# Attention and feed-forward on one core: late q and k loads by row chunks, four more seven-product blocks, and a written order for the first batch

## The chip, the cores and the metric

The kernel runs on one core of a Trainium2 chip. The metric is the device time of one execution in microseconds (us), the median of several runs. A profiled execution gives the trace from which all durations are read.

## The reference

For 8 batches of 12 heads with 448 rows of 64, attention without softmax; then a feed-forward block with a gate on all 3584 tokens of width 768, inner width 1536:

```python
scores = scale * np.matmul(q, k.transpose(0, 1, 3, 2))      # scale = 1/sqrt(64)
attn = np.maximum(scores, 0.0) ** 2 / S
attn_out = np.matmul(attn, v)                               # then x = (tokens, heads * 64)
g = x @ w_gate
gelu = 0.5 * g * (1.0 + erf(g * inv_sqrt2))
val = x @ w_val
out = (gelu * val @ w_out).astype(np.float32)
```

Inputs and output are float32 in memory; the kernel computes in bfloat16 with float32 sums.

## The kernel before

The Python program plans the whole kernel first and then writes the instructions in the order of the plan. An `Op` is one step on one engine with a planned cost; `run_plan` takes, at each moment of planned time, the next step that is ready on each engine. The chip does not see the plan: each engine runs its instructions in the order that was written and waits on semaphores.

**Matrix products.** Every matmul uses a quarter of TensorE (PE): 64 rows by 64 columns of weights, so four run side by side, and helper `mm` (L343) writes nearly all of them; they must be told apart by their tiles. The widths of the moving operand are 448 (scores, values, gate and value products), 224 (seven-product blocks and some tails) and 384 (output products).

**Attention of a batch.** Heads are taken in thirds of a batch, m = 0, 1, 2, of four heads, and in pairs `pr`. `load_qk` (DMA issued on POOL, L402) brings q and k into `qk16`, cast to bfloat16; `load_v` (L417) brings v. In batches 0 and 1 PE transposes q and k (`add_transposes`, `add_first_transposes`) and DVE copies the result to `qkT`. From batch 2 on, DVE regroups into `qkr` (L449), and two DMA transposes per third, issued on SP (L454), write `qkT`. `add_scores` writes one of 21 score steps of a batch: scores into `sp`, relu on ACT into `rl` (L685), square on DVE into `attnT` (L697). `add_values` multiplies by v and copies to `xT` (L760). In batch 0 transposes, scores and values are in a fixed order, by times that a formula gives; later attention steps are units that the planner places by a time spread from `lo` to `hi`, which `SHIFT` moves for each batch from 2 on.

**Feed-forward of a batch.** For each 128 of the inner width there is a gate product and a value product (24 matmuls of 448 columns each), gelu on ACT (L1007) and a product on DVE (L1012) into `uT`. In `NPB[b]` blocks of a batch the four products of 256 of the inner width are made by seven products of half the tokens' width instead (`add_pair`, names 1 to 7, 24 matmuls of 224 columns each), with sums of weights `ws` (`add_pair_sums`, L833), sums of tokens `ts` (L857), copies and sums of parts (L925, L929), gelu (L933) and product (L938). Weight sums of blocks 4 and 5 are kept in the room of the load tiles, so they come after the last loads and transposes (`ROOM = 4`). A block's weights are overwritten by a sum when its first batch with seven products is reached, so `NPB` can only grow.

**Output.** Groups of four 64-token chunks, a to n, are made by seven products too (`add_product`, names a1 to n7, 384 columns); results go to `osb` (L1185, L1187) and are stored (L1202) from SP, each 64-row chunk by a DMA of its own. The last tile is stored in two halves of its columns.

**Order.** `LINE` lists the feed-forward work: a digit is a gate or value product of that batch, `3A1` product 1 of block A of batch 3, `a1` output product 1 of group a. The position gives a planned time; a unit is taken as soon as it is ready, in the order of these times.

**Loads.** Late q and k (batch 2 on) come in four loads per third, two heads each; v in four loads too. A load waits for a relu step of an earlier third (`PACE`), and starts only behind a mark in PE's instruction stream, one in every 256 instructions (`gate`, `Blocks`).

Of the kernel before, what the change touches and what calls it, by code (L numbers as in the profile page):

```python
# [9 lines left out]


LINE = """
0 0 0 0 0 0 0 0 0 0 0 0 0 0 0 0 0 0 0 0 0 0 0 0 1 1A1 1 1 a1 1 1 1 1A7 1 1 1A2 1 1A6 1 1 1 1 a6 1 a7
a4 1A5 1 1 1 1A4 1 1A3 a5 a3 1 a2 2 2 2 1 b1 b7 b2 b6 2 b4 c1 2 c6 2 2B1 2 c7 2A7 2 b5 2 c5 2B6 2B2
2A1 2 2B7 2B5 b3 c4 2 2B4 2 3 2A2 2A6 2B3 c3 2A4 2 2A5 2 2A3 3A1 2 3A7 2 d7 3 c2 d1 d6 3A6 3 3 3 4
d5 3 3A2 e1 d2 3 4 3 3A4 d4 3 3B1 e6 3 3B7 e7 3B2 d3 3B6 3 3B4 4A1 3B5 3B3 3A5 4 3 3 3A3 3 3 3 4A6
e4 f1 4A7 e5 f7 e2 f2 4 4A2 4C1 4B1 4 4A5 e3 4C6 f6 4 4B6 4C7 4C2 f5 g1 4 4C5 f4 4B2 4B7 5 4 4B5 g7
4B4 5 g2 4A4 4C4 f3 4A3 4 g6 5A1 5B1 4C3 5 5 4B3 5A7 4 4 5A2 5B7 4 5B2 5 5D1 5D2 5B6 5D7 g5 5C7 5D6
g3 5C1 h1 h2 5D5 5A6 g4 5A5 5D4 h7 5B5 5C6 5C5 5A4 5 5 5B4 5C2 h6 5 5D3 6 5A3 5C4 5C3 6A1 5B3 6A2 i1
i6 h5 i7 6B1 6A6 6B7 i2 i4 6A7 6D1 6B6 6D6 6B2 6 6B5 j1 6D7 j7 h3 h4 6B4 6A4 6D2 6 i5 6A5 6D5 j2 6B3  # L20
j6 6C1 j5 6 6C6 6C2 6D4 6 i3 6C7 6D3 6 6C5 7A1 6A3 7B1 6C4 7B2 6 6 6C3 7A2 7B6 k1 7B7 k2 k6 7A7 k7
7D1 7D7 7C1 l7 l1 7C2 7B4 j4 7C7 k5 7C6 7B5 7D2 7B3 7F1 j3 7C5 k4 7F6 7E1 7E6 7A6 7F2 7D6 7D5 7F7
# [232 lines left out]
def kernel(  # L255
# [10 lines left out]
    nc = tc.nc  # L266
# [31 lines left out]
    SINGLE = "3"  # L298
# [93 lines left out]
    def load_qk(b, i, h0, h1, deps=()):  # L392

        src = (q, k)[i]
        m, r0 = divmod(h0, 4)

        def tile_of():
            if (b, m) not in qk16:
                qk16[b, m] = hpool.tile([128, 4, SC * D], bf16, name="qk16", tag="qk16")
            return qk16[b, m][HALF[i], r0:r0 + h1 - h0, :]  # L400
# [39 lines left out]
    def add_dma_transposes(b, m, deps=()):  # L440


        wait = Op("IDLE", 2.0 if b == EARLY else 5.0, lambda: None,
                  [*deps] + [head_op[b, pr, i] for pr in (2 * m, 2 * m + 1) for i in range(2)])
        IDLE.append(wait)

        def emit_copy():
            qkr[b, m] = lpool.tile([128, SC, 4, D], bf16, name="qkr", tag="qkr")
            nc.vector.tensor_copy(  # L449
                qkr[b, m].rearrange("p c h d -> p h c d"),  # L450
                qk16[b, m].rearrange("p h (c d) -> p h c d", d=D))

        def emit_transpose(i, c0, c1):
            ins = nc.sync.dma_start_transpose(  # L454
                qkT_tile(b, m)[:, c0:c1].rearrange("d c r x -> d (c r) x"),
                qkr[b, m][:, c0:c1].rearrange("p c h d -> p (c h d)"))
# [143 lines left out]
    def add_transposes(at, b, m, rs):  # L600
# [17 lines left out]
                    blocks.add(nc.tensor.transpose(t[HALF[j], c, :], src[:, 2 * r + j, c, :],  # L618
                                                   ident[:, :], tile_position=(0, P * j)))

        def emit_copy(r):
            nc.vector.tensor_copy(qkT_tile(b, m)[:, :, r, :], box[r])

        n, last = next_scores(at) if b else (0, [])
        both_ops = []
        for r in rs:
            if not b:
# [5 lines left out]
            t = t_op[b, m, r] = Op("DVE", 0.54, lambda r=r: emit_copy(r),  # L633
                                   [lo], lag=0.2, prio=1)
            qk_used.setdefault((b, m), []).append(lo)
            t_made.setdefault((b, m), []).append(t)
            DVE.append(t)
            if not b:
                bank_read(box["k", r], t)
            if (b, m, r) == (0, 0, 1):  # L640
# [7 lines left out]
    def add_scores(at, b, u):  # L648
# [31 lines left out]
        alone = b == 0 or u == NU - 1  # L680

        def emit_relu():
            if first:
                duo["rl"] = rpool.tile([128, 2, 2, S], bf16, name="rl", tag="rl")
            relu.ins = nc.scalar.activation(  # L685
                duo["rl"][:, u % 2, :, :], box[0][:, :, 0:S], AF.Relu).ins

        def emit_sq():
            if alone and not first:
                a = duo["a"]  # L690
            else:
                a = duo["a"] = apool.tile([128, 2, 2, S], bf16, name="attnT", tag="attnT")
# [16 lines left out]
        old = duos[n_d - RING_R] if n_d >= RING_R else None  # L709
        relu = Op("ACT", 0.845, emit_relu, [ops[0][-1], ops[1][-1], *(old["sq"] if old else ()), *duo.get("relu", ())],  # L710
                  lag=0.18, prio=2)
        scores_read(n, relu)
# [16 lines left out]
    def add_values(at, b, pr):  # L729
# [44 lines left out]
        x_op[b, pr] = Op("DVE", 0.575, emit_copy, [o_op[b, pr]], lag=0.2, prio=1,  # L774
                         other=("ACT", 0.5, emit_scaled) if b else None)
        DVE.append(x_op[b, pr])
        bank_read(box["k"], x_op[b, pr])
        if last:
            ops[1][0].after = ops[0][1]
# [342 lines left out]
    def add_product(at, gr, name, final):  # L1122
# [73 lines left out]
        (DVE if added else ACT).append(rd)  # L1196
        st["read", name] = rd
        st["read", stage] = rd
        def emit_store(j, engine=nc.sync, part=slice(0, d_model)):
            b, c = chunks[t % 2][j]  # L1200
            rows = out[b * S:(b + 1) * S, :].rearrange("(p c) d -> c p d", c=SC)
            engine.dma_start(rows[c, :, part], osb[t][HALF[j], part])  # L1202

        if name in "2345":
            st["done", t] = [*st.get(("done", t), ()), rd]
            if final and t == t0:
                SP.append(Op("SP", 0.6, lambda: emit_store(0, nc.sync, cols), [rd], prio=-1))
                ACT.append(Op("ACT", 0.1, lambda: emit_store(1, nc.scalar, cols), [rd], prio=-1))
            elif len(st["done", t]) == 2:
                stored[t] = [Op("SP", 0.6, lambda j=j: emit_store(j), st["done", t], lag=2.5, prio=-1)  # L1210
                             for j in range(2)]
# [78 lines left out]
    for b in range(B):  # L1290
# [15 lines left out]
        if b < EARLY:  # L1306
            for m in range(NM):
                for rs in ((0,), (1,)) if b == 0 else ((0, 1),):


                    x = -5.0 if m else -2.0
                    if b == 0:
                        x = (1.5 * step if rs == (1,) else -3.0) - step * (m == NM - 1)
                    t_at = lo + SC * m * step + x
                    if (b, m) == (1, 0):
                        t_at = PLACE5 + 0.05
                    work.append((t_at, 1, add_transposes, (b, m, rs)))
        for pr in range(NPAIR):
            u = SC * (pr // 2) + (VC - 1, SC - 1)[pr % 2]
            x = lo + u * step + max(4.5, (3.2 + 1.5 * (pr == 0) if b == 0 else 2.5) * step)  # L1320
            work.append((PLACE5 if (b, pr) == (0, NPAIR - 1) else x, 2, add_values, (b, pr)))
# [129 lines left out]
```

## Time and profile before

| | |
|---|---|
| median of 3 runs | 404.31 us (404.19 to 406.43) |
| the profiled execution | 406.77 us, span of its instructions 405.0 us |
| granted TensorE clock, mean | 0.996 |
| PE, busy | 391.4 us (97%), 10285 matmuls |
| DVE, ACT, busy | 306.4 us (76%), 254.3 us (63%) |
| DMA | 45.09 MB, 76446 packets |
| gate and value products of 448 columns | 2496 matmuls, 349 ns each (four run side by side) |
| seven products of 224 columns | 3696 matmuls, 256 ns each |
| relu L685 | 168, 920 ns each |

The profiled execution's time is 1.77 us more than its span. A line of a group reads: line, engine, operation, output <- inputs, shapes, count, then busy time, mean of one, and the idle time of the engine ahead of it with what ended that. A matmul's duration is longer than its share of PE's time, because four quarters run at once and matmuls are pipelined; the pace is read from counts in a window.

### The profile page before, as it was taken

Reading aid. Unit: us, or ns where it says so; the run is one execution under the profiler, and the core shown is the slowest. Engines: PE = TensorE matmul, PEld = TensorE weight load, DVE = VectorE, ACT = ScalarE, POOL = GpSimd, SP = SyncE. Lnnn points to the kernel's source line nnn. Section 1 sums busy time; section 2 is a strip of 40 time slices with the busy share of each in tenths; the row PEclk is TensorE's granted clock in tenths of the full one; section 3 lists DMA queues with packets and bytes.
Section 4 is the critical chain, followed back from the end, with each engine's and each line's share of the span. In section 5 each row is a group of like instructions: output and inputs, shape, how many; then the busy total and the mean of one; then the engine's idle time right before and its main releaser. Section 6 shows DMA issues by size and latency. Waiting matters only on the chain.

```text
span 405.0 us, 22382 instructions
## 1 busy us (share of the span) xinstructions
PE 391.4 (97%) x10285; PEld 356.2 (88%) x10285; DVE 306.4 (76%) x540; ACT 254.3 (63%) x389; POOL 115.9 (29%) x192
## 2 busy tenths in 40 slices
PE   7999999999998999999999998999999999999994
PEld 3557788999887799999999998999999999999993
DVE  2885699679867589879887997558889997865671
ACT  5857672376677677577877686537787873444430
POOL 7656314533434343144342442101421000000000
PEclk9999999999999999999999999999999999999998
DMA  7999998989999985989698984621937301111125
GB/s 102 189 199 198 197 210 129 149 109 100 131 151 153 159 107 76 131 127 150 84 142 104 176 146 55 104 68 21 116 58 114 83 3 44 42 42 45 42 62 138
DMA packets 76446, 45.09 MB, mean 111 GB/s; under 512 B 37312, under 2 KB 72896, under 8 KB 76352
## 3 DMA queue, kind: packets, MB, share of 16 engines
q0 software_dynamic: 38304, 24.39, 47.1%
q1 hardware_dynamic: 37888, 19.08, 27.2%
q8 instruction: 80, 1.31, 1.4%
q10 hardware_dynamic: 160, 0.20, 0.2%
q14 instruction: 14, 0.11, 0.1%
HBM read 48.76 MB, written 11.01 MB: 148 GB/s over the span
## 4 chain that ended last, share of the span: by engine, by line
PE 93%; DMA 4%; issue 2%; POOL 1%; DVE 0%; ACT 0%; POOLq 0%
PE ff L343 82%; PE sp L343 8%; DMA qkT<-qkr 3%; PE ff L539 1%; DMA qk<-in_k_dram 1%; PE sp L618 1%; PE ff L618 1%; POOL qk L402 0%; DVE xT L760 0%; DVE attnT L697 0%; ACT osb L1187 0%; POOL ident masks.py:199 0%; POOL ident masks.py:197 0%; POOLq L1435 0%
## 5 line engine op out<-in xcount | busy, mean ns | idle before, releaser
L343 PE MATMUL ff<-xT,wg 64*64 64x448 bf16 (+1 forms) x2304 | 192.1, 306 | 0.2 <-PE ff L343 0.2
L685 ACT ACTIVATE rl<-sp 128x896 bf16<-128x896 f32 x168 | 152.3, 920 | 54.2 <-PE sp L343 47.1
L343 PE MATMUL ff<-xT,wv 64*64 64x448 bf16 x1248 | 143.5, 349 | 1.8 <-issue 1.8
L343 PEld LDWEIGHTS <-wv 64*64 64x64 bf16 x2304 | 128.7, 107 | 8.0 <-issue 2.8
L343 PEld LDWEIGHTS <-wg 64*64 64x64 bf16 x2304 | 126.8, 107 | 7.8 <-issue 2.4
L697 DVE TENSOR_TENSOR attnT<-rl 128x1792 bf16<-128x1792 bf16 (+1 forms) x98 | 92.1, 952 | 8.9 <-ACT rl L685 8.5
L343 PE MATMUL ff<-attnT,v 64*64 64x448 bf16 (+1 forms) x768 | 83.0, 326 | 0.4 <-DVE attnT L697 0.2
L343 PEld LDWEIGHTS <-s 64*64 64x64 bf16 x1344 | 80.7, 107 | 2.3 <-issue 0.2
L417 POOL DMA_DIRECT2D v<-in_v_dram x84 | 50.1, 600 | 109.2 <-ACT rl L685 43.6
L343 PEld LDWEIGHTS <-ws 64*64 64x64 bf16 x1584 | 80.6, 107 | 0.8 <-issue 0.2
L343 PE MATMUL sp<-qkT 64*64 64x448 bf16 (+1 forms) x768 | 76.0, 328 | 1.8 <-DMA qkT<-qkr 0.8
L343 PE MATMUL ff<-ts,wv 64*64 64x224 bf16 x1056 | 68.1, 256 | 2.0 <-issue 2.0
L343 PE MATMUL ff<-ts,ws 64*64 64x224 bf16 x1056 | 66.6, 256 | 0.0
L343 PE MATMUL ff<-wo,s 64*64 64x384 bf16 x672 | 65.4, 323 | 0.0
L343 PEld LDWEIGHTS <-uT 64*64 64x64 bf16 x1008 | 59.9, 107 | 1.4 <-issue 0.2
L343 PE MATMUL ff<-wo,uT 64*64 64x384 bf16 x672 | 60.8, 323 | 0.0
L343 PE MATMUL ff<-wt,s 64*64 64x384 bf16 x672 | 59.3, 322 | 0.0
L929 DVE TENSOR_TENSOR part<-ff,part 128x448 f32<-128x448 f32 x66 | 40.6, 622 | 16.1 <-PE ff L343 14.2
L1012 DVE TENSOR_TENSOR uT<-gel,ff 128x448 bf16<-128x448 bf16 x52 | 32.2, 620 | 23.8 <-PE ff L343 21.2
L925 ACT COPY part<-ff 128x448 f32<-128x448 f32 x66 | 34.7, 533 | 23.6 <-PE ff L343 22.8
L343 PEld LDWEIGHTS <-v 64*64 64x64 bf16 x768 | 45.5, 107 | 4.1 <-issue 1.7
L1187 ACT COPY osb<-ff 128x384 f32<-128x384 f32 x56 | 26.8, 480 | 28.1 <-PE ff L343 27.7
(51 smaller groups left out, 416.8 us busy)
## 6 DMA issues: line engine op xcount, KB each, us to landing
out_dram<-osb SPq DMA_DIRECT2D x54, 192.0 KB, 3.6
v<-in_v_dram POOLq DMA_DIRECT2D x72, 64.0 KB, 3.3
qk<-in_q_dram POOLq DMA_DIRECT2D x38, 112.0 KB, 4.1
qk<-in_k_dram POOLq DMA_DIRECT2D x38, 112.0 KB, 4.4
wg<-in_moe_w_gate_dram POOLq DMA_DIRECT2D x6, 384.0 KB, 10.2
wv<-in_moe_w_val_dram POOLq DMA_DIRECT2D x6, 384.0 KB, 10.9
wo<-in_moe_w_out_dram POOLq DMA_DIRECT2D x4, 576.0 KB, 14.8
v<-in_v_dram POOLq DMA_DIRECT2D x12, 128.0 KB, 6.9
```

The lines of the kernel that those rows point to most:

```text
L343: ins = nc.tensor.matmul(o, lhsT, rhs, start=start, stop=stop, skip_group_check=onto, tile_position=(P * row, P * col))
L417: return nc.gpsimd.dma_start(v16[b, m][HALF[i], h0 % 4:h0 % 4 + h1 - h0, :, :], v[b, h0:h1].rearrange("h (p c) d -> p h c d", c=SC)[:, :, ...
L539: blocks.add(nc.tensor.matmul(t[:, :], warm[:, 0:128], warm[:, :], start=True, stop=True))
L618: blocks.add(nc.tensor.transpose(t[HALF[j], c, :], src[:, 2 * r + j, c, :], ident[:, :], tile_position=(0, P * j)))
L685: relu.ins = nc.scalar.activation(duo["rl"][:, u % 2, :, :], box[0][:, :, 0:S], AF.Relu).ins
L697: nc.vector.tensor_tensor(a[:, part], duo["rl"][:, part], duo["rl"][:, part], op=ALU.mult)
L925: rd.ins = nc.scalar.copy(st["t", name][:, :], box[0][:, 0:S]).ins
L929: rd.ins = nc.vector.tensor_tensor(t[:, :], box[0][:, 0:S], t[:, :], op=ALU.add).ins
L1012: u_op[b, fc].ins = nc.vector.tensor_tensor(uT[b][:, fc, :], gel.pop((b, fc))[:, :], box[0][:, 0:S], op=ALU.mult).ins
L1187: ins = nc.scalar.copy(o, box[0][:, 0:OGS])
```

## The change

Four things change in one step.

- Blocks: `NPB` gives batch 3 three in place of two seven-product blocks, batch 4 four in place of three, and batch 6 six in place of four (batches counted from 0).
- Loads: from batch 2 on, each of q and k comes in two loads per third of a batch, of all four heads, the first with rows 1 to 4 and the second with rows 5 to 7 of each group of seven rows; v comes in two loads of four heads in place of four of two. `PACE` gets shorter with it.
- First batch: `START` writes down the order of transposes `t`, scores `s` and values `v`, in place of the formula. Options to move copies to ACT (a suffix "a") or to square without the relu copy (`DIRECT`) are added but not used: no name has the suffix and `DIRECT` is empty.
- Order: `LINE` and `SHIFT` are new throughout. A tile's two chunks are stored by one DMA where both are of one batch; the last half-tile is stored by one DMA from the queue of ACT or SP.

By the formula the order of the first batch was t00 s0 s1 t01 s2 s3 s4 s5 t10 s6 s7 v0 s8 t11 s9 v1 s10 s11 t20 s12 s13 v2 s14 t21 s15 s16 v3 s17 s18 s19 s20 v4.

```diff
 LINE = """
-0 0 0 0 0 0 0 0 0 0 0 0 0 0 0 0 0 0 0 0 0 0 0 0 1 1A1 1 1 a1 1 1 1 1A7 1 1 1A2 1 1A6 1 1 1 1 a6 1 a7
...
-7A5 7E7 7D4 l6 7C4 k3 7E2 7A4 7F4 7F5 7E4 7C3 7E5 7A3 l2 7E3 7D3 7F3 l5 l4 m1 l3 m6 m2 m7 n1 n6 m5
-n7 n5 n4 m3 n2 m4 n3
+0 0 0 0 0 0 0 0 0 0 0 0 0 0 0 0 0 0 0 0 0 0 0 0 1 2 1 1A1 1 a1 1 1 1 1 2A1 a2 1A2 1A7 1A6 1 a7 1 2
...
+5C5 5 h4 6A1 5D4 5C4 5A3 5C3 5 5D3 6A2 i1 i7 6B1 h3 i6 h2 i5 6A7 i2 6B7 6B2 6C1 6E7 i3 6B6 6D1 6C7
...
+7D5 k3 7C3 7B3 7F5 7A5 l3 7A4 7D3 7F4 l2 7A3 7E3 7F3 m7 m1 m2 n1 m6 n6 n7 m5 m4 m3 n5 n3 n4 l4 n2
 """
-SHIFT = "-138.25 -21.25 -4 -1 9 -147.75 33 -348.25 26.75 -75 3 -0.75"
+START = """
+t00 s0 s1 t01 s2 s3 s4 t10 s5 s6 s7 v0 s8 t11 v1 s9 s10 s11 t20 s12 s13 v2 s14 t21 s15 v3 s16 s17
+s18 s19 v4 s20
+"""
+SHIFT = "-49.75 -46.75 -49.75 0.75 -189 -3.75 -6.25 -13.25 8.25 -103.5 -149.5 -1.75"
-    PACE = 0, 0, 1, 2, 3, 4, 5, 6
+    PACE = 0, 0, 1, 2, 4, 5
+    DIRECT = ()
-    NPB = (0, 1, 2, 2, 3, 4, 4, 6)
+    NPB = (0, 1, 2, 3, 4, 4, 6, 6)
...
-        op = load(4 * (h1 - h0) * S * D, lambda: nc.gpsimd.dma_start(
-            tile_of(), src[b, h0:h1].rearrange("h (p c) d -> p h (c d)", c=SC)),
-            deps, rate=400e3 if b else 300e3)
-        qk_loads.setdefault((b, m), []).append(op)
+            cols = slice(c0 * D, c1 * D)
+            return nc.gpsimd.dma_start(
+                qk16[b, m][HALF[i], r0:r0 + h1 - h0, cols],
+                src[b, h0:h1].rearrange("h (p c) d -> p h (c d)", c=SC)[:, :, cols])
+        for c0, c1, rate in (((0, SC, 400e3 if b else 300e3),) if b < EARLY
+                             else ((0, VC, 390e3), (VC, SC, 350e3))):
+            op = load(4 * (h1 - h0) * P * (c1 - c0) * D, lambda c0=c0, c1=c1: emit(c0, c1), deps, rate=rate)
+            qk_loads.setdefault((b, m), []).append(op)
...
-                  [*deps] + [head_op[b, pr, i] for pr in (2 * m, 2 * m + 1) for i in range(2)])
+                  [*deps, *qk_loads[b, m]])
...
+    placed0 = {x.rstrip("ad"): -60.0 + 0.8 * n for n, x in enumerate(START.split())}
...
-        def emit_store(j, engine=nc.sync, part=slice(0, d_model)):
-            b, c = chunks[t % 2][j]
+        (b, c), (b_, c_) = chunks[t % 2]
+        pieces = [(b, c, 2, slice(0, 2 * P))] if b == b_ else [(b, c, 1, HALF[0]), (b_, c_, 1, HALF[1])]
+        def emit_store(b, c, n, at, engine=nc.sync, part=slice(0, d_model)):
-            engine.dma_start(rows[c, :, part], osb[t][HALF[j], part])
+            engine.dma_start(rows[c:c + n, :, part], osb[t][at, part])
...
-            for h in (4 * m, 4 * m + 2):
-                load_qk(b, i, h, h + 2)
+            load_qk(b, i, 4 * m, 4 * m + 4)
-            for h in (4 * m_, 4 * m_ + 2):
-                load_v(b_, h, h + 2)
+            load_v(b_, 4 * m_, 4 * m_ + 4)
...
-                    t_at = lo + SC * m * step + x
+                    t_at = placed0[f"t{m}{rs[0]}"] if b == 0 else lo + SC * m * step + x
...
+            if b == 0:
+                x = placed0[f"v{pr}"] if pr < NPAIR - 1 else PLACE5
+            work.append((x, 2, add_values, (b, pr)))
...
-            work.append((lo + u * step, 3, add_scores, (b, u)))
+            work.append((placed0[f"s{u}"] if b == 0 else lo + u * step, 3, add_scores, (b, u)))
```

More of the change, by code (lines that the diff above doesn't have):

```diff
@@ L12 @@
 LINE = """
-0 0 0 0 0 0 0 0 0 0 0 0 0 0 0 0 0 0 0 0 0 0 0 0 1 1A1 1 1 a1 1 1 1 1A7 1 1 1A2 1 1A6 1 1 1 1 a6 1 a7
[L14 to L22, printed above, removed]
@@ L23 @@
-7A5 7E7 7D4 l6 7C4 k3 7E2 7A4 7F4 7F5 7E4 7C3 7E5 7A3 l2 7E3 7D3 7F3 l5 l4 m1 l3 m6 m2 m7 n1 n6 m5
-n7 n5 n4 m3 n2 m4 n3
-"""
-SHIFT = "-138.25 -21.25 -4 -1 9 -147.75 33 -348.25 26.75 -75 3 -0.75"
+0 0 0 0 0 0 0 0 0 0 0 0 0 0 0 0 0 0 0 0 0 0 0 0 1 2 1 1A1 1 a1 1 1 1 1 2A1 a2 1A2 1A7 1A6 1 a7 1 2
+a6 1 1A5 1A4 1 1 a5 1A3 a4 1 2A2 1 1 1 1 1 2 a3 2 1 1 c1 b1 2 b7 b2 2A7 c6 c7 c5 2 2 c2 2B1 b6 2B7
+2A6 b4 c3 b5 2 c4 2B6 b3 2B5 2A4 2 2 2A5 2 2 3A1 2 2B2 2A3 2B4 2B3 2 2 3B7 3 3B1 2 3A2 d7 d1 3B6 3A6
@@ new lines @@
+3B2 3A7 d2 3 3C1 3 d6 3C6 d5 3B4 d4 e1 3 d3 3A5 3 3B5 3 3C7 3 3C2 e7 3 3B3 3A4 3 3 3 3 3C5 4A1 3C4
+3C3 3A3 f7 4A2 f1 f6 4A7 4C1 4 e6 f5 4C7 e5 e2 4A6 f2 4C2 4B1 g7 e4 4 4 4D1 4B2 4B7 f4 g1 4B6 4 4 f3
+e3 g6 4A5 4C6 4D7 4C4 4 4D6 4 4B5 4C5 4 4D2 4D4 4B4 4A4 4D5 g4 4A3 5B1 4B3 4C3 4D3 5 5B7 5A1 5B2 5A6
+g5 g2 5 h1 5B6 5 h7 5 5A7 5A5 5B5 g3 5B4 5A2 5C1 5D1 h6 5D6 5A4 5C2 5D7 5 5B3 5D2 5C7 5C6 5D5 h5 5
+5C5 5 h4 6A1 5D4 5C4 5A3 5C3 5 5D3 6A2 i1 i7 6B1 h3 i6 h2 i5 6A7 i2 6B7 6B2 6C1 6E7 i3 6B6 6D1 6C7
@@ new lines @@
+6D7 6C2 6A6 6B5 6A4 6D2 6C6 6D6 i4 6A5 6F7 6E1 6D4 6E2 6E6 6C5 j1 6F1 j2 6E5 6F6 6D5 6C4 6D3 j7 6B4
+6F2 7E1 6E4 6A3 6F4 6B3 6E3 6F5 j6 j4 6C3 6F3 7A1 k1 k7 k6 7E6 7A7 k2 7E2 7E7 7E4 7B1 7A2 l7 7C1 7E5
+k4 7C2 k5 7B7 7A6 j5 7B6 j3 7B2 7C7 7F1 7C6 l1 7C5 7F7 l6 7D1 7D6 7F2 7D7 7C4 7F6 l5 7B5 7D2 7B4 7D4
+7D5 k3 7C3 7B3 7F5 7A5 l3 7A4 7D3 7F4 l2 7A3 7E3 7F3 m7 m1 m2 n1 m6 n6 n7 m5 m4 m3 n5 n3 n4 l4 n2
+"""
+START = """
+t00 s0 s1 t01 s2 s3 s4 t10 s5 s6 s7 v0 s8 t11 v1 s9 s10 s11 t20 s12 s13 v2 s14 t21 s15 v3 s16 s17
@@ L395, in load_qk, with emit @@
         m, r0 = divmod(h0, 4)
-        def tile_of():
+        def emit(c0, c1):
             if (b, m) not in qk16:
                 qk16[b, m] = hpool.tile([128, 4, SC * D], bf16, name="qk16", tag="qk16")
-            return qk16[b, m][HALF[i], r0:r0 + h1 - h0, :]
-        op = load(4 * (h1 - h0) * S * D, lambda: nc.gpsimd.dma_start(
-            tile_of(), src[b, h0:h1].rearrange("h (p c) d -> p h (c d)", c=SC)),
-            deps, rate=400e3 if b else 300e3)
-        qk_loads.setdefault((b, m), []).append(op)
+            cols = slice(c0 * D, c1 * D)
[6 more added lines that the diff above has]
+            qk_loads.setdefault((b, m), []).append(op)
         for pr in range(h0 // 2, h1 // 2):
@@ L619, in emit, with emit_copy @@
                                                    ident[:, :], tile_position=(0, P * j)))
-        def emit_copy(r):
-            nc.vector.tensor_copy(qkT_tile(b, m)[:, :, r, :], box[r])
+        def emit_copy(r, on_act):
+            (nc.scalar.copy if on_act else nc.vector.tensor_copy)(qkT_tile(b, m)[:, :, r, :], box[r])
         n, last = next_scores(at) if b else (0, [])
@@ L632, in add_transposes @@
             hi.after = lo
-            t = t_op[b, m, r] = Op("DVE", 0.54, lambda r=r: emit_copy(r),
-                                   [lo], lag=0.2, prio=1)
+            mine = b == 0 and f"t{m}{r}a" in START.split()
+            t = t_op[b, m, r] = Op("ACT" if mine else "DVE", 0.85 if mine else 0.54,
+                                   lambda r=r, mine=mine: emit_copy(r, mine), [lo], lag=0.2, prio=1)
             qk_used.setdefault((b, m), []).append(lo)
             t_made.setdefault((b, m), []).append(t)
-            DVE.append(t)
+            (ACT if mine else DVE).append(t)
             if not b:
@@ L682, in emit_relu @@
         def emit_relu():
-            if first:
+            if "rl" not in duo:
                 duo["rl"] = rpool.tile([128, 2, 2, S], bf16, name="rl", tag="rl")
@@ L686, in emit_relu, with duo_tile @@
                 duo["rl"][:, u % 2, :, :], box[0][:, :, 0:S], AF.Relu).ins
+        def duo_tile():
+            if "a" not in duo:
+                duo["a"] = apool.tile([128, 2, 2, S], bf16, name="attnT", tag="attnT")
+            return duo["a"]
         def emit_sq():
[L689 to L692, printed above, removed]
+            a = duo_tile()
             for i, keys in enumerate(duo["of"]):
@@ L709, in add_scores, with emit_direct @@
         old = duos[n_d - RING_R] if n_d >= RING_R else None
+        def emit_direct():
+            a = duo_tile()
+            for key in keys:
+                att[key] = a[:, u % 2]
+            s = box[0][:, :, 0:S]
+            nc.vector.scalar_tensor_tensor(a[:, u % 2], s, 0.0, s, op0=ALU.max, op1=ALU.mult)
+        if b == 0 and u in DIRECT:
+            keys = duo["of"][-1]
+            sq = Op("DVE", 1, emit_direct, [ops[0][-1], ops[1][-1]], lag=0.2, prio=2)
+            scores_read(n, sq)
+            duo.setdefault("sq", []).append(sq)
+            sq_list.append(sq)
+            for key in keys:
+                sq_of[key] = sq
+            DVE.append(sq)
+            both(at, zip(*ops))
+            return
         relu = Op("ACT", 0.845, emit_relu, [ops[0][-1], ops[1][-1], *(old["sq"] if old else ()), *duo.get("relu", ())],
@@ L772, in emit_scaled @@
             nc.scalar.activation(x_tile(), box[0][:, 0:S], AF.Copy, scale=out_scale)
-        x_op[b, pr] = Op("DVE", 0.575, emit_copy, [o_op[b, pr]], lag=0.2, prio=1,
-                         other=("ACT", 0.5, emit_scaled) if b else None)
-        DVE.append(x_op[b, pr])
+        if b == 0 and f"v{pr}a" in START.split():
+            x_op[b, pr] = Op("ACT", 0.5, emit_scaled, [o_op[b, pr]], lag=0.2, prio=1)
+            ACT.append(x_op[b, pr])
+        else:
+            x_op[b, pr] = Op("DVE", 0.575, emit_copy, [o_op[b, pr]], lag=0.2, prio=1,
+                             other=("ACT", 0.5, emit_scaled) if b else None)
+            DVE.append(x_op[b, pr])
         bank_read(box["k"], x_op[b, pr])
@@ L1206, in add_product @@
             if final and t == t0:
-                SP.append(Op("SP", 0.6, lambda: emit_store(0, nc.sync, cols), [rd], prio=-1))
-                ACT.append(Op("ACT", 0.1, lambda: emit_store(1, nc.scalar, cols), [rd], prio=-1))
+                if engine == "ACT":
+                    ACT.append(Op("ACT", 0.5, lambda: emit_store(*pieces[0], nc.scalar, cols), [rd], prio=-1))
+                else:
+                    SP.append(Op("SP", 0.6, lambda: emit_store(*pieces[0], nc.sync, cols), [rd], prio=-1))
             elif len(st["done", t]) == 2:
-                stored[t] = [Op("SP", 0.6, lambda j=j: emit_store(j), st["done", t], lag=2.5, prio=-1)
-                             for j in range(2)]
+                stored[t] = [Op("SP", 0.6, lambda piece=piece: emit_store(*piece), st["done", t], lag=2.5, prio=-1)
+                             for piece in pieces]
                 SP.extend(stored[t])
@@ L1311 @@
                     x = -5.0 if m else -2.0
-                    if b == 0:
-                        x = (1.5 * step if rs == (1,) else -3.0) - step * (m == NM - 1)
-                    t_at = lo + SC * m * step + x
+                    t_at = placed0[f"t{m}{rs[0]}"] if b == 0 else lo + SC * m * step + x
                     if (b, m) == (1, 0):
@@ L1319 @@
             u = SC * (pr // 2) + (VC - 1, SC - 1)[pr % 2]
-            x = lo + u * step + max(4.5, (3.2 + 1.5 * (pr == 0) if b == 0 else 2.5) * step)
-            work.append((PLACE5 if (b, pr) == (0, NPAIR - 1) else x, 2, add_values, (b, pr)))
+            x = lo + u * step + max(4.5, 2.5 * step)
+            if b == 0:
+                x = placed0[f"v{pr}"] if pr < NPAIR - 1 else PLACE5
+            work.append((x, 2, add_values, (b, pr)))
         for u in range(NU):
-            work.append((lo + u * step, 3, add_scores, (b, u)))
+            work.append((placed0[f"s{u}"] if b == 0 else lo + u * step, 3, add_scores, (b, u)))
     work.sort(key=lambda w: w[:2])
```

## The prediction

> **What bounds the kernel now.** I read the page first (busy times, the chain that ended last), then what TensorE (PE) waited for, then 10 us windows of all engines, and last the places where PE stood still. Page of the kernel before:
>
> ```profile
> span 405.0 us, 22382 instructions
> PE 391.4 (97%) x10285; PEld 356.2 (88%) x10285; DVE 306.4 (76%) x540; ACT 254.3 (63%) x389; POOL 115.9 (29%) x192
> PE 93%; DMA 4%; issue 2%; POOL 1%; DVE 0%; ACT 0%; POOLq 0%
> ```
>
> PE is the bound: 93% of the chain is PE's own work. So a change pays if it takes matmul work away, or standstills of PE; work of VectorE (DVE) or ScalarE (ACT) costs nothing as long as it stays under PE. What PE waited for (total us, times, longest):
>
> ```profile
> PE ff L343 <- issue: 3.8, 3, 1.8
> PE sp L343 <- DMA qkT<-qkr: 0.8, 1, 0.8
> PE sp L343 <- issue: 0.5, 1, 0.5
> ```
>
> These 3.8 + 0.8 + 0.5 = 5.1 us are the standstills after the start. The two long ones, in the timeline (the bracket is the idle time before):
>
> ```profile
> 131.96 1.21 SPq L454 DMA_TRANSPOSE qkT<-qkr  x1
> 132.22 0.37 PE L343 MATMUL ff<-xT,wv 64*64 64x448 bf16 x1 [1.80 <-issue]
> ...
> 242.93 1.22 SPq L454 DMA_TRANSPOSE qkT<-qkr  x1
> 244.38 0.25 PE L343 MATMUL ff<-ts,wv 64*64 64x224 bf16 x1 [1.65 <-issue]
> ```
>
> "issue" says that no semaphore held PE. Page part 3 has 80 packets, 1.31 MB, of an instruction queue (16 KB each, so 256 instructions of 64 bytes; PE has 2 x 10285); its packet records show one fetch at 129.71, 0.71 us ahead of the first standstill's start, after a gap of 8.2 us from the one before, and one at 241.47 that took 1.49 us where 1.0 is usual. I read these standstills as late instruction fetches beside DMA traffic. That is a reading, not shown.
>
> **The change, part by part.**
>
> *Seven-product blocks.* NPB goes from a sum of 22 to 26. Each of the four replaces 4 gate or value products of 24 matmuls of 448 columns (96) by 7 of 24 matmuls of 224 (168). Two stretches of one kind each, for the pace of one (busy us, count):
>
> ```profile
> 206.70:211.40 4.70, 4.70 (x107) 4.52 (x103) 1.00 0.84 165
> 268.50:270.00 1.50, 1.50 (x71) 1.50 (x65) 1.00 0.00 0
> ```
>
> The count holds every matmul that touches the window, so one's duration (0.35 and 0.26 us, from the groups) is added: (4.70 + 0.35)/107 = 47.2 ns at 448 columns and (1.50 + 0.26)/71 = 24.8 ns at 224. One block: 96 x 47.2 - 168 x 24.8 = 4.53 - 4.17 = 0.36 us; four: 1.5. If 224 columns ran at the pace per column of the first row, 23.6 ns, it would be 0.57 each, 2.3 for four. I take **-1.9**, ends -1.5 and -2.3. Hidden work: per block ACT gets 3 copies of 533 ns and two gelus for two (+1.6 us), DVE 3 adds of 622 and two products for two (+1.9 us): +6.5 us ACT, +7.5 us DVE in all, behind PE as long as DVE is not full where they fall (a rival below).
>
> *Line, SHIFT.* All of the order of gates, seven-products, output products and of attention is new. Same products, so no work; but each DMA transpose (36 stay), load and store now falls elsewhere on PE's line. Late v loads go from 72 to 36, late q/k loads stay 72, stores from 58 to 33 (both chunks of a tile in one where they are of one batch): 238 such transfers become 177. Batch 3's attention gets lo 22 in place of 50 in planner units, ahead of the place where PE waited 0.8 us for the transposes of batch 2. The 5.1 us of standstills can vanish, stay or grow: ends -5.1 and +2.6 (half as much again). With a quarter fewer transfers and the one DMA wait pulled apart I take half of them gone: **-2.6**.
>
> *Row chunks.* Late q and k: four loads of 2 heads, 128 rows of 896 bytes as written, become four of 4 heads, 256 rows of 512 or 384 bytes. Issue cost on POOL is the same (L402 600 ns whether 112 or 224 KB). In the packet records after 60 us, 9216 packets of 896 bytes took 114 ns each, 9216 of 512 bytes 75 ns. The line through both gives 61 ns for 384 bytes: 9216 x (75 + 61 - 114)/16 = 12.7 us more of every DMA engine between 60 and 310 us; at 75 ns for both 20.7 us. Spread over 72 loads that is 0.2 to 0.3 us later landing on 4.1 to 4.4. Of 18 groups of transposes one reached PE, so the cover holds 17 of 18 times: **+0.2**; ends 0 and +0.8 (that one wait a second time). All four loads were waited for before the regrouping copy, and still are. The v loads wait for relu 4 and 5 in place of 3 to 6: nothing.
>
> The page "DMA: Bandwidth & Descriptors" of the Trainium skill (Specifications) speaks against this part: pieces below 512 B fall off line rate because of a read-modify-write. By it the 384-byte pieces gain nothing over the 512-byte ones, which is the 20.7 us end above. The trace of before has no 384-byte load that could show it.
>
> *Start.* Order of batch 0: t10 ahead of s5, v1 ahead of s9, v3 ahead of s16, v4 ahead of s20; no "a" suffix and an empty DIRECT, so no work moves to another engine. ACT's 21 relus set this stage:
>
> ```profile
> 6.93 6.32 ACT L685 ACTIVATE rl<-sp 128x896 bf16<-128x896 f32 x7 [0.48 <-PE sp L343]
> 13.61 2.59 ACT L685 ACTIVATE rl<-sp 128x896 bf16<-128x896 f32 x3 [0.37 <-PE sp L343]
> 16.59 9.38 ACT L685 ACTIVATE rl<-sp 128x896 bf16<-128x896 f32 x11 [0.38 <-PE sp L343]
> ...
> 10.93 0.38 PE L343 MATMUL sp<-qkT 64*64 64x448 bf16 x4
> 11.38 0.58 PE L618 MATMUL ff<-ident,qk 128*64 128x128 bf16 x14
> ```
>
> At best both gaps close: -0.75. But the k load of heads 4 to 7 lands at 11.25 by its semaphore, and t10 (L618 at 11.38) runs right behind it. Put ahead of s5, it holds s5 from 10.93 to 11.9, and relu s5 then starts at about 12.4 instead of 11.4; the 0.37 gap behind it is partly used up: up to +1.0. I take **+0.3**.
>
> *Stores and tail.* Half as many issues on SP, off PE's path; the last half-tile goes out as one DMA of 128 rows on one queue in place of two of 64 on two. They landed in 2.8 and 3.1 us; ends -0.6 (an issue less) and +0.6. **-0.3**.
>
> **Sum:** -1.9 - 2.6 + 0.2 + 0.3 - 0.3 = -4.3. The profiled execution took 406.77 (span 405.0 and 1.77 around it), so 402.5; the median of the runs shown is 404.31, 2.46 below it, and from it **400.0**.
>
> **Rivals.**
>
> 1. *All standstills go* (25%): -1.9 - 5.1 + 0.2 = -6.8, 397.5; with the products' good end and the start's gaps closed 395.7. For it: they are three events and a DMA wait in 400 us, not a steady cost. Against: nothing in the change aims at instruction fetch, and 4 x 72 more matmuls with as many weight loads are 576 instructions, 2 more fetches.
>
> 2. *Only the products* (15%): standstills come back as large elsewhere: 404.31 - 1.9 + 0.2 = 402.6. For it: transposes and fetches stay what they are. The page "Runtime: NRT & Kernel Launch" of the Trainium skill (Instruction fetch mechanics) calls a 16 KB crossing mostly hidden; by that it makes no time either way, and the two standstills above would be something else.
>
> 3. *Slower: DVE becomes the bound at 290 to 330 us* (15%). There it has almost no room left:
>
> ```profile
> 290.00:300.00 10.00, 8.72 (x15) 1.00 0.52 76
> 300.00:310.00 10.00, 9.28 (x24) 1.00 0.77 123
> 310.00:320.00 10.00, 9.36 (x16) 1.00 0.35 71
> 320.00:330.00 10.00, 9.43 (x16) 1.00 0.08 24
> ```
>
> First use of weight blocks 4 and 5 moves from batch 7 to 6. Their 8 weight sums (L833, 552 ns, last in DVE's priority) lie between 313.5 and 351.8 and can't start before the last transposes (issued at 302.8, landing 4.9) because they take the room of the load tiles. In the new line 6E7, which needs the last sum, stands 80 us of planned PE work ahead of the end, about 312 us with 8 us of attention still to come. So 4.4 us of sums and 3.7 us of the two extra blocks' DVE work press into 300 to 330: 28.1 + 8.1 = 36.2 us in 30, PE waits 6.2 us: 404.31 - 1.9 + 6.2 + 0.3 = 408.9. DVE begins to bind when more than 30 - 28.1 = 1.9 us is added to that stretch; the kernel is slower than before once PE's wait passes what the products save, 1.9 us. Against: DVE is at 22.0 of 30 us from 330 to 360, and SHIFT for the last batch goes from +3 to -149.5, which pulls its loads and attention forward.
>
> **Chances.** Forecast 45% (own range 397.5 to 402.6), of which 28 lie below 400.3, which is 1% faster (1% is about what a measurement of this kernel can tell from no change); rival 1 25, all faster; rival 2 15, same; rival 3 15, slower. Faster 0.53, same 0.32, slower 0.15. The range takes rival 1's low end and runs to where slower begins: 395.7 to 408.4; outside it stay most of rival 3 and a few hundredths below.
>
> **What would show it.** Right: gate and value matmuls of 448 columns 384 fewer and of 224 columns 672 more; PE waits for issue and qkT at 1 to 4 us in all; first relu chain a little later than 25.97; last PE at about 395. Wrong: PE waiting for DVE or "part" between 290 and 330 (rival 3); PE waits of 5 us or more (rival 2); PE busy down by more than 3 us (products mis-sized); qk landing above 5 us (chunks mis-sized).

## Result and profile after

The changed kernel takes 523.59 us (median of 4 runs, 521.2 to 524.08); the kernel before, run beside it, takes 404.74 us. The ratio is **1.2916, 95% interval 1.2859 to 1.2973**: 29% slower. Medians are of all runs; ratios leave out single runs that took over 1.5% longer than the fastest of the same kernel. Its profiled execution took 523.93 us, span 521.9 us. The forecast was 400.0.

The page of the changed kernel, the three lines that were shown of before:

```profile
span 521.9 us, 22868 instructions
PE 414.8 (79%) x10570; PEld 372.1 (71%) x10573; DVE 313.6 (60%) x552; ACT 261.4 (50%) x401; POOL 96.8 (19%) x156
PE 76%; issue 14%; DMA 5%; ACT 1%; SPq 0%; DVE 0%; ACTq 0%
```

DVE and ACT are as busy as their added copies and sums make them (+7.2 and +7.1 us; the prediction had +7.5 and +6.5). PE's products came as counted too (10570 matmuls in the trace, 10573 by the forecast). What is new is that PE stands still. What it waited for (total us, times, longest):

```profile
PE ff L350 <- issue: 54.0, 13, 9.6
PE sp L350 <- issue: 15.7, 2, 8.9
PE ff L350 <- ACT osb L1223: 8.7, 3, 4.2
```

"issue" was 3.8 us before, longest 1.8. The third line is new: the copies into `osb` wait for a free buffer, and PE for the copies. Both stand in the chain that ended last (start, length, what):

```profile
108.48 4.51 issue
114.48 11.35 DMA out_dram<-osb
...
142.34 9.11 issue
...
164.60 9.62 issue
...
473.55 14.32 DMA out_dram<-osb
```

A store into `out_dram` had no place in the chain before. Where the time is lost, by stages (window, length, busy us and count of PE, PEld, DVE, ACT, POOL, granted clock, DMA share, GB/s):

```profile
50.00:100.00 50.00, 50.00 (x1185) 46.98 (x1179) 40.38 (x68) 26.41 (x41) 14.87 (x25) 1.00 0.99 137
100.00:150.00 50.00, 32.61 (x709) 27.07 (x701) 24.56 (x45) 21.46 (x31) 9.08 (x15) 0.90 1.33 91
...
300.00:350.00 50.00, 34.71 (x895) 32.55 (x895) 25.41 (x43) 21.53 (x32) 7.34 (x12) 0.83 0.81 69
350.00:400.00 50.00, 38.80 (x1127) 37.59 (x1125) 31.84 (x57) 28.41 (x46) 3.06 (x5) 0.93 0.59 50
400.00:450.00 50.00, 49.93 (x1698) 48.45 (x1693) 41.15 (x79) 27.09 (x49) 0.00 (x0) 1.00 0.12 41
450.00:522.00 72.00, 40.49 (x1158) 36.34 (x1146) 24.36 (x51) 17.14 (x34) 0.00 (x0) 0.81 0.13 47
```

Read the edges. Until 100 us nothing is lost; the first store is issued at 95.7. From 400 to 450 nothing is lost although stores go out; the last DMA transpose is issued at 378.4. So the larger part of the loss lies where stores **and** transposes are both under way: PE idles 72.8 us between 100 and 400 (the same sum before, 100 to 350: 4.9). The loads end there too, the last one issued at 373.0; the experiments come back to that. A second part comes after 450, with no transpose left: PE idles 31.4 us (before, after 350: 5.9). There the merged stores take longer than their tiles come, PE waits for a free `osb`, and the last store ends at 520.5, 23.0 us after PE's last matmul (before: 4.0 us after it). PE's busy time is 23.4 us longer, at granted clocks of 0.81 to 0.93 in the stages with long idle stretches. 67.9 + 25.5 + 23.4 = 116.8 us: the whole difference of the spans, 116.9.

SP's queue in one of the standstills, the one that the chain shows at 142.34:

```profile
135.91 1.18 SPq L1240 DMA_DIRECT2D out_dram<-osb  x2
137.19 10.71 SPq L464 DMA_TRANSPOSE qkT<-qkr  x1
```

The same issue took 1.21 us in the timeline of before. The packet records tell what lay ahead of it. The two chunk stores of a tile have 128 packets of 3072 bytes. Before, where no load ran beside them (from 314 us on), they took 1.7 to 2.5 us in all, with 9 to 14 packets under way on average (156 to 231 GB/s). The one store that takes their place also has 128 packets, but only **about two under way at a time** (on average 1.6 to 2.0 beside transposes, 2.0 without). It lasts 7.6 to 8.8 us where it is least disturbed (45 to 52 GB/s) and up to 11.5 beside others. In the standstill above, the store ends at 150.94. From 143 to 150 no packet of a transpose moves, and 7 to 13 packets of loads do in each microsecond; in the microsecond from 151 on the transposes move 557.

Beside the store at 256.77 to 267.00 transposes run from 257.74 to 268.67; an instruction fetch comes at 268.60 and ends at 269.71; PE, still since 263.95, goes on at 271.19. So it goes nine times for over 3 us between 100 and 400: seven of these standstills end 1.3 to 1.6 us after a 16 KB fetch has ended, and where a store lay ahead the fetch starts 0.8 to 2.9 us after the store's last packet. The other two (from 142 and from 216) hold no such fetch and end 0.4 to 0.5 us after the store's last packet.

Two under way at a time fits two DMA engines. The 4-byte packets of completions say the same. Queue q10 carries what ACT issues: 128 rows of the last half-tile and their completions. Before (two stores of 64 rows), after (one of 2 x 64):

```profile
q10 hardware_dynamic: 160, 0.20, 0.2%
```

```profile
q10 hardware_dynamic: 130, 0.20, 0.1%
```

160 = 128 + 2 x 16, and 130 = 128 + 1 x 2. On SP's queue q1 the count falls from 37888 to 37168: 56 stores with 16 completions each are 896, and 24 with 2 plus 8 with 16 are 176; the difference, 720, is what is missing. The store writes `rows[c:c + 2]` of a view "c p d", an access pattern with the 2 chunks outermost, against 128 partitions. The Trainium skill, page "DMA: Bandwidth & Descriptors" (Why a DMA increments its semaphore by 16 and not by 1), states that a DMA runs on the largest number of engines, up to 16, that divides the slowest dimension of both its patterns, sizes of 1 left out, and that each engine used posts one completion: 2 here, 16 for 64 rows. The counts agree.

### The profile page after: what moved, and what is told of

The parts are those of the page before. It is cut to its first block, busy times and chain, and to the rows that moved or that the text cites. A ratio compares the mean times of both kernels' runs of the same rounds, so it can differ in the third digit from the quotient of the medians.

```text
span 521.9 us, 22868 instructions
## 1 busy us (share of the span) xinstructions
PE 414.8 (79%) x10570; PEld 372.1 (71%) x10573; DVE 313.6 (60%) x552; ACT 261.4 (50%) x401; POOL 96.8 (19%) x156
## 3 DMA queue, kind: packets, MB, share of 16 engines
q1 hardware_dynamic: 37168, 19.08, 36.4%
## 4 chain that ended last, share of the span: by engine, by line
PE 76%; issue 14%; DMA 5%; ACT 1%; SPq 0%; DVE 0%; ACTq 0%
PE ff L350 66%; PE sp L350 7%; DMA out_dram<-osb 5%; PE ff L549 1%; PE ff L1420 1%; PE ff L628 1%; PE sp L628 1%; ACT rl L696 0%; ACT osb L1223 0%; PE ff L591 0%; ACT gel L1043 0%; ACT qkT L599 0%; SPq L464 0%; DVE warm L335 0%; ACTq L1223 0%
## 5 line engine op out<-in xcount | busy, mean ns | idle before, releaser
L350 PE MATMUL ff<-xT,wg 64*64 64x224 bf16 (+1 forms) x2304 | 190.1, 309 | 9.5 <-issue 9.5
L350 PE MATMUL ff<-xT,wv 64*64 64x448 bf16 x1056 | 126.5, 364 | 1.9 <-issue 1.9
L350 PEld LDWEIGHTS <-ws 64*64 64x64 bf16 x1872 | 97.1, 110 | 7.5 <-issue 6.7
L350 PE MATMUL ff<-ts,ws 64*64 64x224 bf16 x1248 | 81.3, 266 | 12.9 <-issue 12.9
L350 PE MATMUL ff<-ts,wv 64*64 64x224 bf16 x1248 | 86.0, 268 | 0.0
L350 PE MATMUL ff<-wo,uT 64*64 64x384 bf16 x672 | 68.4, 342 | 12.4 <-issue 12.4
L961 ACT COPY part<-ff 128x448 f32<-128x448 f32 x78 | 41.1, 535 | 56.9 <-PE ff L350 55.5
L965 DVE TENSOR_TENSOR part<-ff,part 128x448 f32<-128x448 f32 x78 | 47.6, 623 | 32.4 <-ACT part L961 16.4
L350 PEld LDWEIGHTS <-qkT 64*64 64x64 bf16 x768 | 40.3, 110 | 25.6 <-issue 22.8
L427 POOL DMA_DIRECT2D v<-in_v_dram x48 | 29.6, 621 | 147.7 <-ACT rl L696 71.0
L1223 ACT COPY osb<-ff 128x384 f32<-128x384 f32 x56 | 26.8, 481 | 58.3 <-PE ff L350 43.4
## 6 DMA issues: line engine op xcount, KB each, us to landing
wv<-in_moe_w_val_dram POOLq DMA_DIRECT2D x6, 384.0 KB, 11.5
```

Source lines behind the costliest of these rows:

```text
L350: ins = nc.tensor.matmul(o, lhsT, rhs, start=start, stop=stop, skip_group_check=onto, tile_position=(P * row, P * col))
L427: return nc.gpsimd.dma_start(v16[b, m][HALF[i], h0 % 4:h0 % 4 + h1 - h0, :, :], v[b, h0:h1].rearrange("h (p c) d -> p h c d", c=SC)[:, :, ...
L961: rd.ins = nc.scalar.copy(st["t", name][:, :], box[0][:, 0:S]).ins
L965: rd.ins = nc.vector.tensor_tensor(t[:, :], box[0][:, 0:S], t[:, :], op=ALU.add).ins
L1223: ins = nc.scalar.copy(o, box[0][:, 0:OGS])
```

## Experiments

Theory A: the merged store runs on two engines and holds what has to pass them. Rivals: B, the new order of work or the new loads put transposes and fetches in each other's way, and the store is merely there; C, the store is slow but harms only by its place ahead of transposes in SP's queue. Ratios are to the kernel before on the same chip.

### Only the stores undone, and only the stores done

The changed kernel with its stores split again, the last half-tile's too:

```diff
-        pieces = [(b, c, 2, slice(0, 2 * P))] if b == b_ else [(b, c, 1, HALF[0]), (b_, c_, 1, HALF[1])]
+        pieces = [(b, c, 1, HALF[0]), (b_, c_, 1, HALF[1])]
```

> The changed kernel with one thing undone: each 64-row chunk is stored by a DMA of its own again. Theory A (a merged store writes an access pattern whose outermost size is 2, runs on few DMA engines, and the instruction fetches and transposes that share those engines wait): the PE issue waits of 69.7 us fall below 8 us, the granted clock goes back to 0.99 or more, time 396 to 405 us. Theory B (line, SHIFT and the extra blocks): time stays above 500 us. Theory C (the 384-byte load pieces): stays above 500 us, q landings stay at 8 us and more.

Measured: 406.59 us, 1.0003 [0.9967, 1.0039]; theory A had expected 396 to 405.

The kernel before with the change's stores (`pieces`, `emit_store`, the last half-tile) and nothing else:

```diff
-            engine.dma_start(rows[c, :, part], osb[t][HALF[j], part])
+            engine.dma_start(rows[c:c + n, :, part], osb[t][at, part])
```

> The kernel before with the merged stores alone. Theory A: 490 to 540 us, PE issue waits of 50 us or more in pieces of up to 10 us, clock near 0.9. Theories B and C: within 1% of before, 404 us.

Measured: 492.95 us, 1.2111 [1.2047, 1.2176]. PE's first wait in each, split stores first:

```profile
PE ff L350 <- issue: 3.1, 8, 1.0
```

```profile
PE ff L343 <- issue: 54.8, 8, 12.2
```

B falls: one edit off takes all of the loss away, and the same edit alone brings 85 us to the old order with the old loads. The other 33 us of the change hang on this edit too, in another order of work: without it that order loses nothing.

### The same store cut by rows

Does the number of engines decide, or the size of the store? In the kernel before each chunk's store is cut in two, so there are more and smaller DMAs and the same bytes; only the row counts differ:

```diff
-            engine.dma_start(rows[c, :, part], osb[t][HALF[j], part])
+            for r0, r1 in ((0, 62), (62, P)):        # or 48, or 56
+                engine.dma_start(rows[c, r0:r1, part], osb[t][P * j + r0:P * j + r1, part])
```

> The kernel before, every store of 64 rows cut into two DMAs of 62 and 2 rows. Nothing is merged. Theory A, by the count of engines: 62 and 2 rows both allow only 2 engines, so the same bytes go through 2 engines as in the changed kernel: well above 450 us. If instead the size of a store (384 KB in one) or the two row blocks in one DMA are what hurts: within 2% of the cut at 48 rows.

> Control for the cut at 62 rows: two DMAs of 48 and 16 rows, both numbers multiples of 16. As many DMAs, as many bytes. Theory A: 402 to 410 us. If it is the number of stores that hurts: as slow as the cut at 62 rows.

> The kernel before, stores cut at 56 rows (56 and 8, both multiples of 8 and not of 16: 8 engines each by the count of completion packets). Between the cut at 48 (16 engines, 403.5 us) and at 62 (2 engines, 514 us): 192 KB over 8 engines takes twice as long as over 16, so 403 to 412 us; the completion packets on ScalarE's queue 32 in place of 64.

| rows | packets on q1, q10 | completions of one pair | time, ratio |
|---|---|---|---|
| 64 (before) | 37888, 160 | 16 (one store) | 1 |
| 62 + 2 | 37216, 136 | 4 | 513.95, 1.2643 [1.2570, 1.2716] |
| 56 + 8 | 38224, 172 | 22 | 404.56, 0.9966 [0.9927, 1.0004] |
| 48 + 16 | 38784, 192 | 32 | 403.51, 0.9942 [0.9908, 0.9976] |

The third column is worked out: q10 has 128 rows and two pairs, so (172 - 128) / 2 = 22; q1 has 56 pairs, so 22 = (38224 - 37888 + 896) / 56. 62 + 2 gives 2 and 2, 48 + 16 gives 16 and 16, and 56 + 8 gives 22 = 14 + 8: 14 divides 56. Its expectation counted 8 for each, which was wrong by that rule of the Trainium skill itself (32 expected on q10, 44 came). The parts of 22 can be told from each store's semaphore events: 15 for a store of 56 rows and 9 for one of 8, and 3 for 62 rows, for 2 rows and for the merged store. That is nearly always one more than the rule's engines where these are fewer than 16; a store of 16, 48 or 64 rows has 16. These four kernels and the merged store follow "the largest divisor up to 16", and the time follows the engines, not the size: stores cut into 190 KB and 6 KB on two engines each cost 26%, cut into 172 KB on fourteen and 24 KB on eight they cost nothing. Twice as many issues on SP cost nothing either.

### Merged stores only after the last transposes

```diff
-        pieces = [(b, c, 2, slice(0, 2 * P))] if b == b_ else ...
+        pieces = [(b, c, 2, slice(0, 2 * P))] if b == b_ and t >= 16 else ...
```

> The kernel before with merged stores only for tiles 16 to 27, whose stores lie behind the last DMA transpose (302.8 us in the trace of before). Theory A1 (a merged store hurts by what is queued behind it: transposes on the same SP queue take 10 us to issue, and the fetches of TensorE's instructions stand still with them): within 2% of before, 400 to 410 us, PE issue waits below 8 us. Theory A2 (a store on 2 engines alone holds up the fetch): PE issue waits of 15 us or more between 305 and 400 us, time 420 us or more.

Measured: 420.45 us, 1.0383 [1.0331, 1.0436]. PE's wait and two windows:

```profile
PE ff L343 <- issue: 2.2, 2, 1.2
```

```profile
320.00:330.00 10.00, 10.00 (x304) 9.77 (x298) 9.60 (x17) 8.45 (x14) 0.00 (x0) 1.00 0.07 28
...
400.00:410.00 10.00, 0.00 (x0) 0.00 (x0) 0.00 (x0) 0.00 (x0) 0.00 (x0) 0.61 0.38 86
```

The same slow stores, 7.6 to 9.0 us each, and PE is full beside them from 316 to 380 us. So the slow store alone is not enough for a standstill. This run does not part transposes from loads, which end with them; other stores on record do. With loads and no transpose beside a slow store PE is full: in the next run below at 358.36 to 367.74 (370 packets of loads, two fetches), and in the changed kernel at 224.61 to 233.16, where the last transpose packet comes at 224.72 (585 packets of loads, two fetches). With transposes and no load beside it, in the changed kernel at 365.52 to 374.40, no fetch comes between 365.74 and 375.20, and PE stands from 372.82 to 378.43. So it takes a transpose beside the store. The expectation was right on PE and wrong on the time: it left out the tail, where the stores, slower than their tiles come, end at 416.5 us, 18.5 us after PE.

### Merged stores from ACT's queue

```diff
-                stored[t] = [Op("SP", 0.6, lambda piece=piece: emit_store(*piece), st["done", t], lag=2.5, prio=-1)
+                stored[t] = [Op("ACT", 0.6, lambda piece=piece: emit_store(*piece, nc.scalar), st["done", t], lag=2.5, prio=-1)
...
-                SP.extend(stored[t])
+                ACT.extend(stored[t])
```

> The kernel before with merged stores, issued from ScalarE's queue in place of SP's, so no transpose stands behind a store in its queue. Theory A1 in its narrow form (the order in SP's queue): 400 to 425 us, with what the issues cost ScalarE. If it is the engines that stores and transposes share, whatever the queue: 450 us or more, and transposes on SP still take several us to issue.

Measured: 485.0 us, 1.1953 [1.1882, 1.2024]. PE's waits, and the transposes' issues on SP (min/median/max ns):

```profile
PE ff L343 <- issue: 28.4, 8, 6.7
PE sp L343 <- DMA qkT<-qkr: 9.2, 1, 9.2
```

```profile
L454 SPq DMA_TRANSPOSE qkT<-qkr x36: 1211/1240/3085, 73.0 to 355.1; - x36
```

For the merged stores on SP, in the run above, the same line is

```profile
L454 SPq DMA_TRANSPOSE qkT<-qkr x36: 1211/1523/13697, 70.9 to 363.0; - x36
```

Out of SP's queue, the long issues are gone (13.7 us to 3.1; 2.7 in the kernel before), against the expectation for shared engines, and half of PE's "issue" time with them. Most of the loss stays, 485.0 us in place of 492.95: PE now waits 9.2 us for one transpose itself. C as the whole cause falls; the place in SP's queue is a part of it. Transposes beside a store in another queue are late all the same, and what the two still share is the DMA engines. That is an argument: the records do not name the engine of a packet.

### What the rest of the change is worth

With split stores, one other part at a time was put back:

```diff
-    NPB = (0, 1, 2, 3, 4, 4, 6, 6)          # old blocks: products 3C, 4D, 6E, 6F as four plain ones in LINE
+    NPB = (0, 1, 2, 2, 3, 4, 4, 6)
...
-t00 s0 s1 t01 s2 s3 s4 t10 s5 s6 ...        # old start: START in the formula's order
+t00 s0 s1 t01 s2 s3 s4 s5 t10 s6 ...
...
-    PACE = 0, 0, 1, 2, 4, 5                 # old loads: also load_qk, load_v by two heads
+    PACE = 0, 0, 1, 2, 3, 4, 5, 6
```

Old blocks:

> The changed kernel with the stores split again and, besides, the block counts of before: in the new line the seven tokens of each of blocks 3C, 4D, 6E and 6F are replaced by four plain ones (at the places of tokens 1, 3, 5 and 7). If four blocks save 1.5 to 2.3 us on TensorE: 1.5 to 2.3 us slower than with split stores alone (406.6 us, ratio 1.0003), so ratio 1.004 to 1.006. If denser instructions eat the saving: the same ratio or lower.

Old start:

> The changed kernel with split stores and the first batch in the order of the formula. By the prediction the new order holds score step 5 behind a load that lands at 11.25 us and costs 0.3 us (up to 1.4): so 0.3 to 1.4 us faster than split stores alone (ratio 1.0003), ratio 0.997 to 1.000; the relu chain of the first batch ends at about 26.0 us in place of 27.4. If the new order is the better one: ratio above 1.0003.

Old loads:

> The changed kernel with split stores and the late q, k and v loads of before (2 heads, whole rows; four v loads). By the prediction the row chunks cost 0.2 us (0 to 0.8): ratio 0.998 to 1.000. If the small pieces feed the many short waits for issue seen with split stores (3.7 us in 9): those shrink and the ratio falls to 0.995 or below.

| with split stores | ratio to before |
|---|---|
| all else as changed | 1.0003 [0.9967, 1.0039] |
| old blocks | 1.0112 [1.0068, 1.0157] |
| old start | 1.0329 [1.0284, 1.0373] |
| old loads | 1.0012 [0.9985, 1.0039] |

Old loads change nothing that can be told. The other two are slower, but neither is the price of the part alone. The plan is made again from the new costs, and its later order shifts with it: with the old start PE is busy 22.5 us after 390 us, where the changed order has 9.6, and its granted clock there is 0.77. That is another tail; that it comes of a `LINE` made for other blocks and another start is a reading. Single prices of blocks and start stay open.

### Towards a faster version

Old start, old loads and the 48 + 16 cut together, on the split stores; then the cut alone, on the split stores:

> Four extra blocks, new line and SHIFT, with the first batch and the late loads of before, and every store of 64 rows cut into 48 and 16 rows as in the control that measured 0.994. If the three are additive: 0.990 to 0.996. If the planner's order is thrown off by what it wasn't searched with: 1.00 to 1.01.

> The changed kernel with split stores (1.000), each cut into one of 48 and one of 16 rows as in the control on the kernel before (0.994). If the cut's gain carries over: 0.992 to 0.997 of the kernel before. If that gain was of that run alone, or belongs to the order before: 1.000, give or take 0.004. By the theory of the engine count both pieces run on 16 engines, so nothing above 1.004.

Measured: 414.76 us, 1.0229 [1.0184, 1.0273], and 407.07 us, 1.0020 [0.9993, 1.0048]. The first is slower than both of its expectations and has the old start's tail again (PE busy 19.4 us after 390 us). The second shows that the cut's 0.6% does not carry over to the changed order. In the order before, PE's waits for issue are 1.8 us in 2 with the cut and 3.8 in 3 without it. The kernel before with its stores cut 48 + 16, at 0.9942, is the only one here that beats both kernels, by an amount whose cause wasn't settled.

## Why the prediction was wrong

**The step that failed is "Stores and tail".** It reads "Half as many issues on SP, off PE's path" and puts the edit at -0.3 us with ends of 0.6 on each side. It counted issues, and priced the merged store by two old ones that landed in 2.8 and 3.1 us. Both of these were 64-row stores on 16 engines. The trace of before had no store with another outermost dimension, so nothing in it gave a price for the merged one, and the working carried the nearest rows over without a bound for that. What the runs put in its place: 85 us in the old order, 118 us in the new, with 45 to 52 GB/s for a store in place of 156 to 231. The rule of the Trainium skill that the result section names stands on the page that the prediction cites for the row chunks. Its "off PE's path" failed as well: PE needs the 36 transposes, and these share SP's queue and, as argued above, the DMA engines with the stores, so PE stood still for up to 9.6 us at a time.

**Row chunks** (+0.2, qk landing above 5 us means mis-sized). In the changed kernel the four loads land in 5.0, 9.7, 8.5 and 8.7 us, but with split stores in 3.6 to 4.7, so the merged stores did that. Old loads against new are 1.0012 to 1.0003, which fits 0.2 us and can't tell it from nothing. By the warning of the Trainium skill, page "DMA: Bandwidth & Descriptors" (Specifications), the prediction let the smaller pieces take as long as the larger at worst. With split stores the late 384-byte packets took 58.5 ns and the 512-byte ones 72.4, which is 7% fewer bytes per nanosecond for the smaller ones; the estimate had 61 to 75.

**Seven-product blocks** (-1.9). The counts came as said: 384 fewer of 448 columns, 672 more of 224. The price per matmul is less sure than the sum made it. Two windows of 224-column work in the kernel with split stores:

```profile
319.40:320.90 1.50, 1.50 (x73) 1.50 (x66) 1.24 (x3) 1.44 (x4) 0.00 (x0) 1.00 0.21 49
323.20:326.30 3.10, 2.95 (x120) 2.70 (x115) 2.57 (x5) 2.70 (x6) 0.00 (x0) 1.00 0.03 9
```

By the prediction's own reading that is (1.50 + 0.26) / 73 = 24.1 ns and (2.95 + 0.26) / 120 = 26.8 ns. A block breaks even at 96 x 47.2 / 168 = 27.0 ns. The stretch that the prediction took, 24.8, was one of the good ones; at the pace of the second window a block gains almost nothing. PE's busy time in all is 391.4 us with split stores, as before, and 389.3 with split stores and old loads: single executions differ by as much as the gain of 1.9 us that was forecast, so these runs do not show whether it came.

**Line, SHIFT** (-2.6, half of 5.1 us of standstills gone). With split stores PE's waits after the start are 3.1 + 0.6 us for issue and 0.7 for ACT, 4.4 in ten pieces, none above 1.0. The two long ones are gone as hoped, and short ones stand in their place: -0.7, not -2.6. The sum of all but the stores, forecast at -4.0 us, is 0.1 us by 1.0003, with 1.5 us either way. So without the stores the forecast would have missed too: about 1.9 us of that is the standstills, and where the rest went is open.

**Start** (+0.3). The first relu chain ends at 27.38 with split stores, 25.97 before; with the old start 27.00 and with the old loads 26.76. "A little later" holds; how much of it is the order can't be told from the loads' own scatter.

**Rivals.** DVE as the bound at 290 to 330 us did not come: with split stores DVE is busy 35.3 of these 40 us, 36.8 before, and PE, which has no wait for DVE after the start, is busy 39.4. One of the four windows:

```profile
300.00:310.00 10.00, 10.00 (x322) 9.82 (x317) 9.45 (x22) 6.22 (x11) 0.00 (x0) 1.00 0.17 42
```

It was the only rival on the slow side, and none had the store in it. PE waits of 5 us or more, the sign of rival 2, came without rival 2. The range's low end, 395.7, does not follow from the terms named for it: -2.3 - 5.1 + 0.2 - 0.75 = -7.95, which gives 396.4. The remark that PE's "issue" time is late instruction fetches beside DMA traffic was a reading; the changed kernel speaks for it in seven of nine long standstills, which end 1.3 to 1.6 us after a fetch; the two long ones of before end 1.4 and 1.5 us after theirs (129.71 + 0.99 to 132.22, 241.47 + 1.49 to 244.38). Why a fetch waits where store and transposes meet, and not beside a slow store alone, no run here shows; nor what PE waited for in the two standstills without a fetch.

## What to carry to other kernels

When two DMAs are made one, look at the outermost dimension of both access patterns before counting what is saved: here 2 in place of 64 cost 29% and saved 25 issues that nobody waited for. In a profile of such a case, divide the completion packets of a queue by its DMAs, and look at how many of one transfer's packets are under way at a time; both tell the number of engines without a timing. (For a queue that also carries other DMAs, take the difference of two kernels, as for q1 above.) And a slow transfer is not off the path because nobody waits for its data: ask what else has to pass the same engines.

## What the runs showed of the hardware

- The completions of a store, and so its number of engines, followed the size of its outermost dimension: 2 for the merged store's 2 chunks, for 62 and for 2 rows, 8 for 8 rows, 14 for 56, 16 for 16, 48 and 64.
- A 384 KB store on two engines, with no transpose beside it, did PE no harm (PE full at 320 to 330 us). Ahead of a DMA transpose it made the issue on SP last 10.7 us in place of 1.2 (13.7 in the old order), and PE stood for up to 12.2 us on "issue". The Trainium skill, page "Runtime: NRT & Kernel Launch" (Instruction fetch mechanics), calls the crossing to the next 16 KB of instructions mostly hidden. If the standstills are late fetches, as read above, it was not hidden here.
- The granted clock fell with PE's idle stretches: 0.66 over 110 to 120 us of the changed kernel, 0.61 over 400 to 410 us of the run with merged stores after the transposes, a stretch without a matmul. PE's busy time was 23.4 us longer with it, so the loss is larger than the waits alone.
